# Attention ahead of routed experts: p times v by column tiles of 64 queries, four of seven key blocks in fp32, maxima in the tile shape of the scores, a new written order

## The chip, the cores and the metric

One core of a Trainium2 chip runs the whole kernel. The metric is the device time of one execution in microseconds, median of three runs. The core's engines are TensorE (PE, with its weight loads PEld), VectorE (DVE), ScalarE (ACT), GpSimd (POOL) and SyncE (SP), which here only issues transfers.

## The reference

Attention over 8 batches, 12 heads, 448 positions, 64 features, with normalized q and k, and then a two-level choice of one of 16 experts for each of the 3584 rows:

```python
q_n, k_n = (rmsnorm(q, g_q), rmsnorm(k, g_k))
scores = np.matmul(q_n, k_n.transpose(0, 1, 3, 2)) / np.sqrt(64)
attn = np.exp(scores - np.max(scores, axis=-1, keepdims=True))
attn = attn / (np.sum(attn, axis=-1, keepdims=True) + 1e-09)
attn_out = np.matmul(attn, v)
...
h = np.maximum(xg[mask_e] @ w1[g, e], 0.0)
ye = h @ w2[g, e]
out[tok_idx] = (g_w * e_w)[:, None] * ye
```

All inputs are fp32. The result must be nearly fp32, so the kernel splits most operands into a high and a low 16-bit part and adds three products (high by high, high by low, low by high).

## The kernel before

**Units.** The attention works on 24 units of four heads (8 batches, 3 units each). The four heads are two pairs: index r says which half of the partitions holds a head's 64 features, index i which half of the columns. A unit's 448 keys are seven blocks: for each i three blocks of 128 keys (0, 1, 2 for i = 0; 4, 5, 6 for i = 1), and block 3, in which the last 64 keys of both i lie one above the other.

**Steps of a unit.** `load` (line 206) brings k, q and v by transfers of SyncE's queue: q in two, k in four, v in six. `plan_prep` (236) squares (ACT), sums (DVE), takes the root and normalizes (POOL or DVE, line 281), transposes q and k on TensorE in fp32 (`tr`, 14 matmuls of 128x128, line 287), and splits them in high and low; for k the high part is taken away by a matmul in PSUM (`sub`, 305). `v_hi` and `v_lo` (320, 324) split v. `plan_max` (375) multiplies the high parts alone, seven times four matmuls of 64 features by 64 queries (line 384), and VectorE takes the row maximum of each (`rd`, 390, 128x896). The 14 columns of maxima are transposed (394), copied with a sign (398) and sent by two small transfers (403) into one row each of a tile `mr`. `plan_scores` (419) forms, for each of seven blocks, four products in PSUM, keys on the partitions: three of the high and low parts and, last, a matmul of a tile `one` with `mr` that takes the maximum away (433 for block 3 with tiles of 64x64, 437 with tiles of 64x128). ScalarE takes the exponential to fp32 p (444). `lo` (449) subtracts from p its upper 16 bits, which are read in place as bf16, and gives an fp16 rest `pl`; VectorE or GpSimd does it.

**Product with v.** `plan_av` (467) has p as the stationary operand, 128 keys by 128 queries, and v, with a 65th column that sums p, as the moving one (line 484). The queries of the two heads of one i are cut in eight pieces (`QUERIES`), one of them doubled where a head ends. For a block it runs three terms: p's upper half by `vh`, the same by `vl`, `pl` by `vh`: 24 matmuls of 65 or 64 columns. `FULL = (1,)` names the blocks that are done in one fp32 term instead (p by `vf`, 8 matmuls, which the trace shows as 16 passes); their p isn't split. Block 3 (`tails`) has 64 keys of each i and uses two row tiles. All add into one PSUM tile `po`, of which there is one. `norm` and `evac` (496 to 501, VectorE) divide, `plan_finish` splits the result (525, 528) and stores it in four transfers (537).

**Order.** Nothing is scheduled at run time: `Flow` (38) collects tasks with their engine, what they depend on and the buffers that they take; a written list `PLAN` (1402) gives each task its place in one order, and a star picks the second of two engines. Each engine obeys that order. `ROOM` (121) says how many buffers of a kind there are. Where `flow.shared` marks tasks, a VectorE task and the GpSimd task behind it are not let run at the same time (84 to 96): the GpSimd one waits.

**Around it.** The stored rows are routed in five groups (transposing transfers at 770, matmuls at 779, small steps to 860). The experts' matmuls (1239, 1266) begin when the attention is nearly done; their weights come by SyncE's queue in 768 KB pieces and are split by ACT and DVE (1179, 1181). Their buffers take the place of the attention's (`m2`, `m3`).

Of the kernel before, what the change touches and what calls it, by code (L numbers as in the profile page):

```python
# [12 lines left out]
F16 = mybir.dt.float16  # L13
BF16 = mybir.dt.bfloat16
# [23 lines left out]
class Flow:  # L38
# [3 lines left out]
    TURNS = ("n", "sq", "ss", "kh", "kl", "qh", "ql", "vf", "vh", "vl", "mx", "mxt", "mr", "po", "xm", "hl", "rx", *(f"st{i}" for i in range(8)), "gb0", "gb1")  # L42
# [65 lines left out]
FULL = (1,)  # L108
# [3 lines left out]
class Attention:  # L112
# [8 lines left out]
    ROOM = dict(n=2, sq=1, ss=1, kh=3, kl=2, qh=3, ql=3, vf=2, vh=2, vl=2, mx=2, mxt=2, mr=2,  # L121
# [3 lines left out]
    TILES = (3, 0, 1, 2, 4, 5, 6)  # L125
    FULL = FULL

    def __init__(self, tc, late, early, out, fin, q, k, v, g_q, g_k, x16):
# [17 lines left out]
        self.ident = t("ident", [P, P], F32)  # L146
        self.i16 = t("i16", [P, P], p=fin)
        self.one = t("one", [P, P])
        self.minus = t("minus", [P, P])
        self.vh = [t(f"vh{j}", [P, 14, 65]) for j in range(R["vh"])]  # L150
        self.pl = [t(f"pl{j}", [P, 2, 512]) for j in range(R["p"])]
        self.ln64 = t("ln64", [P, 1], F32)
        self.mr = [t(f"mr{j}", [P, self.W]) for j in range(R["mr"])]
        self.vf = [t(f"vf{j}", [P, 2, 7, 65], F32) for j in range(R["vf"])]
        self.p = [t(f"p{j}", [P, 2, 512], F32) for j in range(R["p"])]
# [6 lines left out]
    def init(self, j):  # L162
        nc, g = self.nc, self.nc.gpsimd
        f = lambda t: t.bitcast(F32)
        if j == 0:
            g.memset(self.eps, 64e-6 / 1024)
            make_identity(nc, self.ident)
            g.tensor_scalar(self.minus, self.ident, -1.0, None, op0=ALU.mult)
            g.memset(self.ln64, math.log(64.0))
# [3 lines left out]
        elif j == 1:  # L173
            o = self.one.bitcast(F32)
            g.memset(o, 0.0)
            for r in (0, 64):
                g.memset(o[r:r + 1], ONES)
            g.memset(f(self.mr[0]), 0.0)
        elif j == 2:
            g.memset(self.vf[0][:, :, :, 64:65], 1.0)  # L180
            g.memset(self.vh[0][:, :, 64:65], 64.0)
            for p, l in zip(self.p, self.pl):
                g.memset(p[:, 0, 448:512], 0.0)
                g.memset(l[:, 0, 448:512].bitcast(F32), 0.0)
            g.tensor_copy(self.i16, self.ident)
        else:
            for mr in self.mr[1:]:
                g.memset(f(mr), 0.0)
            for vf in self.vf[1:]:
                g.memset(vf[:, :, :, 64:65], 1.0)  # L190
# [15 lines left out]
    def load(self, u, nm, part=None, eng=None):  # L206
# [4 lines left out]
        s = dict(k=self.k, q=self.q, v=self.v)[nm][b, h0:h0 + self.HU].rearrange("(r i) t d -> i r t d", i=2)  # L211
        if nm == "v":
            t = d["v"] = self.vf[u % self.ROOM["vf"]][:, :, :, 0:64]
        else:
            if "n" not in d:
                d["n"] = self.nat.tile([P, 2, 2, 7, self.D], F32, tag="n", name=f"n{u}", bufs=self.ROOM["n"])
            t = d["n"][:, "kq".index(nm)]
# [6 lines left out]
        for i in range(2):  # L224
            if part in (None, i):
                x = s[i][:, 0:self.M].rearrange("r (p c) d -> p r c d", c=3)
                o = t[:, :, 4 * i:4 * i + 3]
                for r in range(2) if nm == "v" else ():
                    eng.dma_start(o[:, r], x[:, r])
# [1345 lines left out]
```

## Time and profile before

| | us |
|---|---|
| median of 3 runs (lowest, highest) | 982.34 (978.81, 988.64) |
| profiled execution | 982.85 |
| its span on the core | 981.2 |
| PE busy | 909.7 (93%) |
| PEld busy | 668.3 (68%) |
| DVE busy | 698.9 (71%) |
| ACT busy | 557.3 (57%) |
| POOL busy | 481.8 (49%) |

The shares are means over the whole span. The attention fills it from the start to about 465 us, the experts fill the rest, and the two have different limits, so the rows below are taken by stretch. A matmul's duration holds its way through the array, and matmuls overlap: what one costs in a stream is the time from its start to the next start. A weight load has its own row (PEld) and can run while earlier matmuls do. The notation 64*128 is the tile shape: rows of the array that are used by columns that are used.

### The profile page before, as it was taken

To read this page: it belongs to the slowest core of one execution; us is meant where nothing else is said; L and a number is where in the kernel's file an instruction comes from. 1 tells how busy PE (TensorE), PEld (TensorE's weight loads), DVE (VectorE), ACT (ScalarE), POOL (GpSimd) and SP (SyncE) were. 2 spreads that over 40 slices of the span, in tenths; PEclk is the share of its full clock that TensorE was granted. 3 is DMA by queue.
4 is the path that set the end of the run, shared out by engine and by line. 5 is a ranking of instruction groups with operands and counts; after the bars stand their busy time and mean duration, and the time that the engine had idled before them with its cause. 6 is when DMAs were issued, how large, how long until landed. Compare 5 with 4: busy or idle time off the path is not lost. (4 is left out here: it accounts for less than half of the span.)

```text
span 981.2 us, 29912 instructions
## 1 busy us (share of the span) xinstructions
PE 909.7 (93%) x12483; PEld 668.3 (68%) x12483; DVE 698.9 (71%) x824; ACT 557.3 (57%) x757; POOL 481.8 (49%) x519
## 2 busy tenths in 40 slices
PE   3899999999999989889989699899999999999996
PEld 1567667676666755557767576677877777788784
DVE  4899898989899987989562385575759455656540
ACT  3678677787766765665441364554646454555330
POOL 5586768786788685962343334133324123221211
PEclk9999999999999998999999799999999999999998
DMA  5334557566676765589998899998999699899510
GB/s 119 97 102 124 125 120 133 130 141 145 135 132 143 146 114 124 149 176 186 262 219 208 152 317 276 349 274 279 311 330 333 201 327 313 265 332 319 156 69 29
DMA packets 234301, 192.81 MB, mean 197 GB/s; under 512 B 156699, under 2 KB 197543, under 8 KB 234162
## 3 DMA queue, kind: packets, MB, share of 16 engines
q1 hardware_dynamic: 226002, 167.36, 65.9%
q0 software_dynamic: 7584, 23.04, 7.6%
q8 instruction: 99, 1.62, 0.7%
q10 hardware_dynamic: 576, 0.46, 0.2%
q14 instruction: 40, 0.33, 0.1%
HBM read 145.69 MB, written 23.41 MB: 172 GB/s over the span
## 5 line engine op out<-in xcount | busy, mean ns | idle before, releaser
L1239 PE MATMUL ps<-mx,w1h 128*128 128x256 f16 (+9 forms) x1728 | 239.9, 257 | 19.2 <-DVE hl L1248 15.9
L1239 PE MATMUL ps<-mx,w1l 128*128 128x256 f16 (+9 forms) x864 | 211.5, 257 | 0.0
L390 DVE TENSOR_REDUCE mx<-pmx 128x2 f32<-128x896 f32 x168 | 177.4, 1083 | 24.9 <-PE pmx L384 23.3
L449 POOL TENSOR_TENSOR pl<-p 128x896 f16<-128x896 f32 x94 | 157.0, 1684 | 62.1 <-DVE pl L449 25.1
L1239 PEld LDWEIGHTS <-w1h 128*128 128x128 f16 x1728 | 157.0, 100 | 33.5 <-issue 17.4
L1266 PE MATMUL ps<-w2h,hh 128*128 128x384 f16 (+2 forms) x768 | 163.8, 304 | 1.7 <-DVE y L1280 1.7
L1266 PE MATMUL ps<-w2l,hh 128*128 128x384 f16 (+2 forms) x768 | 163.8, 303 | 0.7 <-issue 0.7
L1266 PE MATMUL ps<-w2h,hl 128*128 128x384 f16 (+2 forms) x768 | 163.4, 303 | 0.0
L444 ACT ACTIVATE p<-pss 128x896 f32<-128x896 f32 x144 | 128.4, 917 | 61.0 <-PE pss L437 41.7
L1181 DVE SCALAR_TENSOR_TENSOR w1l<-stage,w1h 128x1536 f16<-128x1536 f32 x64 | 110.9, 1752 | 46.0 <-ACT w1h L1179 43.4
L1266 PEld LDWEIGHTS <-hh 128*128 128x128 f16 (+2 forms) x1536 | 101.5, 100 | 60.4 <-issue 7.5
L1248 DVE SCALAR_TENSOR_TENSOR hl<-ps,hh 128x256 f16<-128x256 f32 (+9 forms) x144 | 49.9, 368 | 110.0 <-ACT hh L1246 96.0
L484 PEld LDWEIGHTS <-p 128*128 128x128 bf16 (+1 forms) x2688 | 112.0, 98 | 22.0 <-issue 18.8
L1181 DVE SCALAR_TENSOR_TENSOR w2l<-stage,w2h 128x1536 f16<-128x1536 f32 x64 | 111.4, 1749 | 18.3 <-ACT w2h L1179 18.3
L1228 POOL DMA_INDIRECT xg<-x,tb x41 | 59.9, 1461 | 127.4 <-DMA mx<-xg 99.4
L484 PE MATMUL po<-vh,pl 128*128 128x65 f16 (+1 forms) x1344 | 117.6, 193 | 1.7 <-POOL pl L449 1.5
L484 PE MATMUL po<-vh,p 128*128 128x65 f16 (+1 forms) x1344 | 118.7, 195 | 0.4 <-issue 0.2
L484 PE MATMUL po<-vl,p 128*128 128x64 f16 (+1 forms) x1344 | 117.9, 192 | 0.0
L1179 ACT ACTIVATE w1h<-stage 128x1536 f16<-128x1536 f32 x64 | 92.7, 1478 | 34.4 <-DMA stage<-w 33.9
L1246 ACT ACTIVATE hh<-ps 128x256 f16<-128x256 f32 (+9 forms) x144 | 45.3, 343 | 116.6 <-PE ps L1239 70.2
L1179 ACT ACTIVATE w2h<-stage 128x1536 f16<-128x1536 f32 x64 | 93.7, 1479 | 29.9 <-DMA stage<-w 25.6
L1285 POOL DMA_INDIRECT out<-y,tb x21 | 34.8, 1658 | 152.7 <-ACT y L1278 70.2
(212 smaller groups left out, 1653.1 us busy)
## 6 DMA issues: line engine op xcount, KB each, us to landing
stage<-w SPq DMA_DIRECT2D x64, 768.0 KB
stage<-w SPq DMA_DIRECT2D x64, 512.0 KB
stage<-w SPq DMA_DIRECT2D x64, 256.0 KB
n<-q SPq DMA_DIRECT2D x46, 224.0 KB
n<-k SPq DMA_DIRECT2D x48, 192.0 KB
vf<-v SPq DMA_DIRECT2D x96, 96.0 KB
x<-xhl SPq DMA_DIRECT2D x48, 128.0 KB
x<-xhl SPq DMA_DIRECT2D x48, 96.0 KB
```

Of the source, the lines that this page charges most:

```text
L390: nc.vector.tensor_reduce(d["mx"][:, 2 * g:2 * g + 2], d.pop(("m", g))[:, :, 0:448], axis=AX.X, op=ALU.max)
L444: nc.scalar.activation(p[:, :, 0:448], d.pop(("s", g))[:, :, 0:448], AF.Exp, scale=1.0 / 64, **kw)
L449: ENG[eng].tensor_tensor(l[:, :, 0:448], p[:, :, 0:448], h, op=ALU.subtract)
L484: nc.tensor.matmul(po[:, i, 65 * G:65 * G + n], w, m, start=start and q + j == 0, stop=stop, skip_group_check=True)
L1179: self.nc.scalar.activation(hi, t, AF.Copy, scale=64.0)
L1181: self.nc.vector.scalar_tensor_tensor(lo, t, 64.0, hi, op0=ALU.mult, op1=ALU.subtract)
L1228: self.nc.gpsimd.indirect_dma_start(g[0:m], None, self.x16[0:n], bass.IndirectOffsetOnAxis(ap=tb[0:m, i, 0:1], axis=0), bounds_check=n - 1 ...
L1239: nc.tensor.matmul(s[:, 0:c], wb[w][:, i, fs], x[:, 2 * i + l, o:o + c], start=i + j == 0, stop=i == DC - 1 and j == 2)
L1246: self.nc.scalar.activation(hh, s[:, 0:c], AF.Relu)
L1248: self.nc.vector.scalar_tensor_tensor(hl, s[:, 0:c], 0.0, hh, op0=ALU.max, op1=ALU.subtract)
L1266: nc.tensor.matmul(s[q * m:q * m + m, 0:n], self.h[h][:, f, a:a + m], wb[w][:, f, o:o + n], start=f + j == 0, stop=f == self.FC - 1 and j ...
L1285: i = self.nc.gpsimd.indirect_dma_start(out, bass.IndirectOffsetOnAxis(ap=idx, axis=0), d.pop(("y", i))[:, 0:self.D // r], None, bounds_ch ...
```

## The change

- p by v with a stationary tile of 128 keys by 64 queries; the two heads of one i use the two halves of the array's columns, and of the PSUM partitions. `QUERIES` goes: seven pieces of 64 queries for each head.
- Blocks 3, 0, 1 and 5 are done in fp32 (`FULL`), with a v that is scaled by 64 in a new task `vone` (ACT or POOL, four operations a unit) into a tile `vo`, one buffer; the exponential has no bias for them any more. The order of the blocks is 3, 0, 4, 1, 5, 2, 6.
- Maxima of blocks of 128 queries with tiles of 64x128 (the last with 64x64), their transpose in two matmuls of 64 rows, `mxt` with one buffer; the columns of maxima lie beside the identity matrix.
- Transposes of q and k: 28 matmuls of 64 rows, each half of the partitions into a bank of its own.
- The matmul with the maxima is the first of the four in the scores.
- v and k come in three transfers each, the result goes in two. p's tiles are 448 wide, not 512, without padding to clear.
- `PLAN` is new. Read off it: subtractions `pl` on DVE 18 and on POOL 54 (before 50 and 94); normalizations on DVE 6, on POOL 40 (before 14 and 32, set-up's left out); `vone` on ACT 9, on POOL 15. Some small steps of the expert order are marked as shared.

```diff
-FULL = (1,)
+FULL = (3, 0, 1, 5)
...
-    ROOM = dict(n=2, ..., vl=2, mx=2, mxt=2, mr=2,
+    ROOM = dict(n=2, ..., vl=2, vo=1 if len(FULL) > 1 else 2, mx=2, mxt=1, mr=2,
...
-    TILES = (3, 0, 1, 2, 4, 5, 6)
+    TILES = (3, 0, 4, 1, 5, 2, 6)
...
         def tr(w, a, e):
-            t = d["t", w, a] = self.bank(f"pt{u}{w}{a}", W)
+            t = d["t", w, a] = self.pair(f"pt{u}{w}{a}")[:, :, 0:448]
...
             for g in range(a, e):
-                nc.tensor.matmul(t[:, g * P:g * P + P], n[:, g * P:g * P + P], self.ident, start=g in (a, 4), stop=w == 1,
-                                 is_transpose=True, skip_group_check=True)
+                for h in range(2):
+                    o = slice(64 * h, 64 * h + 64)
+                    nc.tensor.matmul(t[:, h, g * 64:g * 64 + 64], n[o, g * P:g * P + P], self.ident[o, o], start=g == a, stop=w == 1,
+                                     is_transpose=True, skip_group_check=True)
...
+        def v_one(eng):
+            d["vo"] = self.vo[u % self.ROOM["vo"]]
+            for j, g in enumerate(self.FULL):
+                o, x = d["vo"][:, j, :, 0:64], d["v"][:, :, g]
+                if eng == "ACT":
+                    nc.scalar.activation(o, x, AF.Copy, scale=64.0)
+                else:
+                    nc.gpsimd.tensor_scalar(o, x, 64.0, None, op0=ALU.mult)
...
     def plan_max(self, flow, u, B, D):
-            for i in range(2):
+            for i in range(2) if g == 6 else (g // 3,):
                 for r in range(2):
-                    h, o = slice(64 * r, 64 * r + 64), g * P + 64 * i
-                    nc.tensor.matmul(s[64 * i:64 * i + 64, r, 0:448], d["qh"][h, o:o + 64],
-                                     d["kh"][h, 448 * i:448 * i + 448], start=True, stop=True, skip_group_check=True)
+                    h = slice(64 * r, 64 * r + 64)
+                    o, n, w = (64 * i, 64, 448 * i + 384) if g == 6 else (0, P, 448 * i + g % 3 * P)
+                    nc.tensor.matmul(s[o:o + n, r, 0:448], d["qh"][h, w:w + n], d["kh"][h, 448 * i:448 * i + 448], **kw)
...
     def plan_scores(self, flow, u, B, D):
-            for j, (w, m) in enumerate(((d["kh"], d["qh"]), (d["kl"], d["qh"]), (d["kh"], d["ql"]), (None, d["mr"]))):
+            for j, (w, m) in enumerate(((self.one, d["mr"]), (d["kh"], d["qh"]), (d["kl"], d["qh"]), (d["kh"], d["ql"]))):
...
     def plan_av(self, flow, u, B, D):
         def run(g, heads, start=False, stop=False):
-            for q, (G, r, o) in enumerate(self.QUERIES):
-                for j, x in enumerate(zip(*(terms(g, rows, r, o) for _, rows in heads))):
-                    for (i, _), (w, m, n) in zip(heads, x):
-                        nc.tensor.matmul(po[:, i, 65 * G:65 * G + n], w, m, start=start and q + j == 0, stop=stop, skip_group_check=True)
+            for s in range(7):
+                x = [(i, r, terms(g, rows, r, s)) for i, rows in heads for r in range(2)]
+                for j in range(len(x[0][2])):
+                    for i, r, y in x:
+                        w, m, n = y[j]
+                        nc.tensor.matmul(po[self.HALVES[r], i, 65 * s:65 * s + n], w, m, start=start and s + j == 0, stop=stop, skip_group_check=True)
...
         def st():
+            for r, h in enumerate(self.HALVES):
+                nc.sync.dma_start(dst[:, :, 2 * (u % self.UB) + r], d["hl"][h].rearrange("p s l e -> p s (l e)"))
```

## Rows read from the trace of the kernel before

**Rows 1.** Windows by stage: start:end, length, busy us (count) per engine, PEclk, DMA.

```profile
40.00:465.00 425.00, 406.13 (x7375) 283.48 (x7374) 385.99 (x420) 303.19 (x419) 310.58 (x323) 0.98 0.62 135
...
560.00:960.00 400.00, 392.46 (x3905) 304.28 (x3894) 245.74 (x290) 201.07 (x254) 110.06 (x80) 1.00 0.90 276
```

**Rows 2.** Groups on VectorE, 40 to 465 us: count, busy us, mean ns, idle before.

```profile
L390 DVE TENSOR_REDUCE mx<-pmx 128x2 f32<-128x896 f32 x158 | 167.1, 1083 | 23.6 <-PE pmx L384 22.0
L449 DVE TENSOR_TENSOR pl<-p 128x896 f16<-128x896 f32 x50 | 57.5, 1176 | 0.2 <-ACT p L444 0.2
...
L281 DVE TENSOR_TENSOR sq<-n,z 128x896 f32<-128x896 f32 x14 | 15.5, 1107 | 0.5 <-POOL z L275 0.5
```

**Rows 3.** Groups on GpSimd, 40 to 465 us.

```profile
L449 POOL TENSOR_TENSOR pl<-p 128x896 f16<-128x896 f32 x93 | 155.4, 1684 | 54.7 <-DVE pl L449 25.1 <-DVE vl L324 5.9 <-ACT p L444 5.9
L281 POOL TENSOR_TENSOR sq<-n,z 128x896 f32<-128x896 f32 x30 | 50.8, 1700 | 3.6 <-DVE vl L324 1.3 <-DVE sq L281 1.1 <-PE pmx L384 0.3
```

**Rows 4.** Timeline of TensorE around 208 us: start us, duration us, instruction.

```profile
208.14 0.35 PE L437 MATMUL pss<-ql,kh 64*128 64x448 f16 x2
208.33 0.35 PE L437 MATMUL pss<-mr,one 64*128 64x448 f16 x2
208.61 0.38 PE L384 MATMUL pmx<-kh,qh 64*64 64x448 f16 x4
208.93 0.20 PE L484 MATMUL po<-vh,p 128*128 128x65 f16 x1
...
209.03 0.19 PE L484 MATMUL po<-vh,p 128*128 128x65 f16 x1
209.06 0.19 PE L484 MATMUL po<-vl,p 128*128 128x64 f16 x1
```

**Rows 5.** Timeline of TensorE in a tail (block 3).

```profile
214.48 0.19 PE L484 MATMUL po<-vl,p 64*128 64x64 f16 x2
214.51 0.19 PE L484 MATMUL po<-vh,pl 64*128 64x65 f16 x2
```

**Rows 6.** Timeline of one fp32 block: its passes, and its first two loads.

```profile
95.09 1.90 PE L484 MATMUL po<-vf,p 128*128 128x65 f32 x16
...
94.98 0.30 PEld L484 LDWEIGHTS po<-vf,p 128*128 128x128 f32 x2
```

**Rows 7.** Line 484 over the span: duration ns min/median/max.

```profile
L484 PEld LDWEIGHTS po<-vf,p x384: 186/192/193, 45.7 to 460.7; 128*128 128x128 f32 x192
L484 PE MATMUL po<-vf,p x384: 219/275/324, 45.8 to 460.8; 128*128 128x65 f32 x192
```

**Rows 8.** Column tiles in the experts: timeline of sets, and groups of loads.

```profile
538.04 0.26 PE L1266 MATMUL ps<-w2l,hh 128*32 128x192 f16 x4
538.12 0.26 PE L1266 MATMUL ps<-w2h,hl 128*32 128x192 f16 x4
...
L1266 PEld LDWEIGHTS <-hh 128*64 128x64 f16 x352 | 19.6, 111 | 12.3 <-issue 4.8
...
L1266 PEld LDWEIGHTS <-hh 128*32 128x32 f16 x448 | 10.5, 97 | 2.8 <-issue 2.7
```

**Rows 9.** Transposes of q and k: timeline of one unit, and durations in ns.

```profile
212.39 1.75 PE L287 MATMUL pt<-ident,sq 128*128 128x128 f32 x14
...
L287 PE MATMUL pt<-ident,sq x336: 271/273/475, 10.7 to 423.5; 128*128 128x128 f32 x168
```

**Rows 10.** Timeline of GpSimd: an operation of 140 columns.

```profile
379.57 0.44 POOL L793 TENSOR_TENSOR rd<-rl,rm 128x140 f32<-128x140 f32 x1 [3.75 <-DVE rm L791]
```

**Rows 11.** Timelines of SyncE's issues, and of TensorE at the largest hole.

```profile
330.82 2.65 SPq L537 DMA_DIRECT2D x<-xhl  x4
...
342.59 4.13 SPq L229 DMA_DIRECT2D vf<-v  x4
...
364.85 7.50 SPq L770 DMA_TRANSPOSE rx<-x  x2
...
369.16 0.20 PE L779 MATMUL prl<-wrh,rx 128*128 128x20 f16 x1 [2.92 <-DMA rx<-x]
```

More of the change, by code (lines that the diff above doesn't have):

```diff
@@ L297, in hi @@
             kw = dict(scale=self.ghc) if w else {}
-            nc.scalar.activation(d[nm][:, cols(a, e)], d["t", w, a][:, cols(a, e)], AF.Copy, **kw)
+            nc.scalar.activation(cols(d[nm], a, e, w), turned(w, a, e), AF.Copy, **kw)
         def sub(a, e):
-            t, h = d["t", 0, a], d["kh"]
-            for o, z in ((a * P, min(e, 4) * P), (4 * P, e * P)):
-                if a * P <= o < z:
-                    nc.tensor.matmul(t[:, o:z], self.minus, h[:, o:z], start=False, stop=True, skip_group_check=True)
+            for h in range(2):
+                nc.tensor.matmul(d["t", 0, a][:, h, a * 64:e * 64], self.minus, cols(d["kh"], a, e)[:, h],
+                                 start=False, stop=True, skip_group_check=True)
         def lo(w, a, e):
@@ L392, in fin0 @@
+        at = slice(96 - 96 * m, 110 - 96 * m)
         def fin0():
-            t = d["mt"] = self.bank(f"pmt{u}")
-            nc.tensor.transpose(t[0:14, 0:P], d["mx"], self.ident)
+            t = d["mt"] = self.pair(f"pmt{u}")
+            for j in range(2):
+                h = slice(64 * j, 64 * j + 64)
+                nc.tensor.matmul(t[:, j, 0:64], self.ix[h, 64 - 64 * m:192 - 64 * m], self.ident[h, h], start=True, stop=True, skip_group_check=True)
         def fin1():
-            d["mxt"] = self.wl.tile([14, P], F16, tag="mxt", name=f"mxt{u}", bufs=self.ROOM["mxt"])
@@ L530, in st @@
         def st():
-            for r in range(2):
-                f = dst[:, :, 2 * (u % self.UB) + r]
-                for j in range(2):
-                    G = slice(3 * r + (r and not j), 3 + 3 * r + (r or not j))
-                    n, s0 = G.stop - G.start, j if r == 0 else 1 - j
-                    nc.sync.dma_start(f[:, s0:s0 + 2 * n - 1:2], d["hl"][64 * j:64 * j + 64, G].rearrange("p g l e -> p g (l e)"))
+            for r, h in enumerate(self.HALVES):
+                nc.sync.dma_start(dst[:, :, 2 * (u % self.UB) + r], d["hl"][h].rearrange("p s l e -> p s (l e)"))
         x = flow.add("xhi", "ACT", hi, [D["x"]], takes=[B["hl"]], uses=[B["xm"]])
@@ L706, in turn @@
                 o = t[:, 0:S].rearrange("f (p s) -> f s p", s=7)
-                for k in range(3):
-                    nc.tensor.matmul(o[:, 2 * k + c:2 * k + c + 2], hl[:, 4 * c + k, l], self.i16, start=True, stop=True, skip_group_check=True)
-                h, s = slice(64 * c, 64 * c + 64), 0 if c else 6
-                nc.tensor.matmul(o[:, s:s + 1], hl[h, 3, l], self.i16[h, h], start=True, stop=True, skip_group_check=True)
+                h = slice(64 * c, 64 * c + 64)
+                for s in range(7):
+                    nc.tensor.matmul(o[:, s], hl[h, s, l], self.i16[h, h], start=True, stop=True, skip_group_check=True)
             def ev(eng, l, c):
```

382 lines of the change are left out of this document (197 added, 185 removed), and 39 rows, old and new, of the table PLAN.

## The prediction

> **What bounds the kernel now.** I read the windows by stage first, then the groups of VectorE and GpSimd in the attention stretch, then TensorE's timeline inside single units. The stretch from 40 to 465 us holds nearly all of the 24 attention units, 425 / 24 = 17.7 us each. TensorE has matmuls in flight for 406 of its 425 us and VectorE is busy for 386 (91%), ScalarE for 303, GpSimd for 311 [rows 1]. From 560 to 960 us the experts' matmuls run with TensorE at 392 of 400 us [rows 1]; the change leaves them alone, and the weights behind them are asked for only after the attention's routing is done. So what the attention stretch loses, the whole loses, and nothing is won elsewhere except by a better or worse hand-over between the two.
>
> In the attention stretch two engines are nearly full at once. VectorE's list is led by the 158 maxima (167 us), and 50 subtractions that split p into two fp16/bf16 parts cost it 57.5 us and 14 normalizations 15.5 us [rows 2]; GpSimd does the other 93 subtractions (155 us) and 30 normalizations [rows 3]. TensorE is read by start-to-start steps, since matmuls overlap. A set of score or maxima matmuls of 448 columns takes 0.19 us (208.14 to 208.33), and where the next set has another tile shape the step is 0.28 or 0.32: a change of shape costs about 0.1 us [rows 4]. Along the written order TensorE changes shape 316 times up to the last product with v, some 32 us.
>
> **The change part by part, per unit of four heads.**
>
> *Product of p and v, before.* A three-term block is 24 matmuls at a step of 0.03 us (209.03 to 209.06) [rows 4], 0.72; five of them are 3.6. The tail is 24 pairs of row tiles at the same 0.03 [rows 5], 0.72. The one fp32 block is 16 passes that last 1.90 us from the first start to the last end; less the 0.275 of the last, that is a step of 1.625 / 15 = 0.108, or 1.73 for the block [rows 6, 7]. Sum 6.05 us.
>
> *What the fp32 pass waits for.* Two of its weight loads lie 0.30 - 0.19 = 0.11 us apart [rows 6, 7], which is the step of the passes. Its matmuls last 219 ns where the weights were already there, 275 in the run of the block and 324 where nothing was loaded ahead [rows 7]. So the load of 128 fp32 columns (0.108) is the price, and the stream of 65 columns alone is shorter: a fp16 matmul of 65 columns shows 0.19 at a step of 0.03 [rows 4], the fp32 one with its weights there 0.03 more, so about 0.057.
>
> *After.* The stationary tile is 128 keys by 64 queries, in two column tiles side by side, so a three-term block is 42 matmuls or 21 pairs, a fp32 one 28 passes or 14 pairs, and the fp32 tail 14 quadruples (two row by two column tiles). A load of half the columns should take half, 0.054, and then load and stream are equal. If the two tiles of a pair run side by side, a fp32 block costs 14 x 0.058 = 0.81 us, and a three-term block 21 x 0.03 = 0.63. Four fp32 blocks (the tail among them) and three others: 3.25 + 1.89 = 5.14 us, 0.91 less than before. That column tiles do run side by side is seen in the experts: four tiles of 32 columns with 192 streamed columns go at 0.08 us a set (538.04 to 538.12), the time of one of them, with four weight loads in each set [rows 8]. A load of 64 columns lasts 111 ns against 97 for 32 [rows 8], so 64 take some 28 ns and stay under the 30 of the stream. Bounds: 5.14 if all of it is parallel, 9.9 or 8.2 in the rivals below. I take the low end, because the nearest rows are those of column tiles.
>
> *Transposes of q and k.* Before, 14 fp32 transposes at (1.75 - 0.273) / 13 = 0.11 us [rows 9], 1.54. After, 28 of 64 rows, two side by side in different banks, each streaming 64 columns rather than 128: 14 x 0.058 = 0.81 if the stream is what costs, 1.54 if it isn't. Their load is not the price: this step of 0.11 is what 128 columns of stream need at the 0.057 per 65 found above. I take 0.81, 0.73 less.
>
> *Maxima and scores.* The maxima become two matmuls of 128 queries by 64 features where there were four of 64, in the shape of the scores; a set still streams 448 columns, 0.19. The reduction on VectorE reads the same 896 columns (1.083) [rows 2]. Putting the row of the maxima first in each score set means that the first set of a unit waits for its small transfer before three steps that ran ahead of it; at most 3 x 0.19 = 0.57 us a unit, 14 us in all, and nothing where the transfer has landed. I take nothing, since sets of two units interleave in the order.
>
> *Changes of shape.* Maxima, scores and transposes now share 64x128, but p and v left 128x128, which the routing and the subtraction keep: counted along the new order 324 changes, 8 more, 0.8 us. I price the new pairs of shapes as the old ones.
>
> So TensorE loses 0.91 + 0.73 = 1.64 us a unit, 24 x 1.64 = 39 us.
>
> *VectorE and GpSimd.* The three further fp32 blocks need no split of p. The written order has 18 subtractions on VectorE and 54 on GpSimd, where it had 50 and 94; 6 normalizations on VectorE for 14. VectorE: 32 x 1.176 + 8 x 1.107 = 46.5 us less [rows 2], 386 to 340. GpSimd: 40 x 1.684 = 67 less, 8 normalizations x 1.70 = 14 more [rows 3], and the new scaling of v for the fp32 blocks, 15 units x 4 operations of 128 columns; a GpSimd operation of 140 columns takes 0.44 [rows 10], so at most 26: 311 to about 284. ScalarE takes the other 9 units, 9 x 4 at up to 0.44 = 16 on top of 303. Neither becomes the bound. The single buffer of scaled v makes the next unit's scaling wait for the fifth of seven blocks; at least nine TensorE tasks, four blocks of scores of 4 x 0.19 us among them, lie between there and its first use, over 3 us for four operations of 0.44. Uncovered it would be 1.8 us a unit.
>
> *Queue of SyncE.* Per unit it issues v in six transfers, four of which took 4.13 us here, and the stores in four that took 2.65 [rows 11]; after, v in three and the stores in two. The queue was not the bound over the stretch, but it made the largest hole: two transposing transfers held it from 364.85 for 7.5 us, and TensorE stood for the routing's x at 369.16 with 2.92 us idle [rows 11]. Fewer issues can only shorten that; I count nothing for it.
>
> *Sum.* TensorE gives up 39 us and VectorE 46, so the stretch can follow TensorE: 425 - 39 = 386, at which TensorE would have the same small slack as now and VectorE 340 / 386 = 88%. With 1 us for shapes and the set-up, the span falls from 981.2 to 942, and the profiled execution from 982.85 (0.5 us over the median of the three runs, 982.34) to 943. If TensorE is fed better because the other engines have more room, the 19 us of the stretch without matmuls can go too, 924 at best. If the slack grows instead, since four engines now lie between 284 and 386 us, I allow 20 us: 963.
>
> **The rivals.**
>
> *Loads of column tiles don't hide.* If a tile's load can't run beside the matmul of its neighbour in the same rows, a pair costs load plus stream: 0.058 in fp16, 0.111 in fp32, so 3 x 21 x 0.058 + 4 x 14 x 0.111 = 9.9 us, 3.8 more than before. With the transposes' 0.73 that is 3.1 x 24 = 74 us, about 1057. Against it stand the sets of four column tiles at 0.08, where four loads are hidden [rows 8]; for it, that none of those has fewer than 192 streamed columns to hide behind. The Trainium skill, page "TensorE: Matmul & The Clock Gate", Part 3, The mechanism, speaks for this rival: a weight load overlaps a running matmul only when its group of rows differs, and two column tiles have the same rows. By that rule the time is this rival's; the experts' sets disagree with it. Chance 0.07.
>
> *A fp32 pass has its price whatever its width.* If 0.11 belongs to the pass and not to its 128 columns, a block of 14 pairs costs 1.57 and the product 4 x 1.57 + 1.89 = 8.2 us, 2.1 more. Less 0.73 for the transposes, 1.4 x 24 = 33 us slower, 1016: slower than before from a price of 0.087 a pair on (4 x 14 x 0.087 + 1.89 + 0.81 = 7.6, the old sum). For it: every pass in the run of a block takes 0.108 to 0.112. Against it: the 219 and 324 ns matmuls, which only a load explains. Chance 0.07.
>
> *The engines are lighter, the order is not.* TensorE obeys one order; holes such as that at 362 to 372 us come from waits that no sum of loads shows. If new ones of that kind eat most of the 39 us, 966 to 990; and if the change doesn't make VectorE's work shorter where it counts, the time ends here too. For it: VectorE's idle 39 us of now. Chance 0.14.
>
> **How the numbers follow.** The forecast has 0.72, with its own 920 to 965 (924 and 963, and a little for what the set-up and the hand-over move). A run of this kernel can tell about 1% from no change, 973 to 993. Faster by over 1%: 0.72 and a third of the third rival, 0.77. Within: 0.08. Slower: the first two rivals and a remainder, 0.15. The range must leave out no more than 0.2: 920 to 985 leaves the first two rivals, the end of the third and what is below 920.
>
> **What would show it.** Right: fp32 matmuls of 128x64 at 0.06 us a pair; three-term pairs at 0.03; transposes two in 0.06; VectorE's subtractions down to 18 and its busy time in the attention stretch near 340; the last product with v near 425 us instead of 465, and about 516 us from there to the end as now. Wrong: fp32 pairs at 0.11 or fp16 pairs at 0.06; a stretch that stays at 425 us with VectorE idle for far more than 50; or an end that doesn't follow because the hand-over to the experts waits longer.

## The result and the profile after

The changed kernel takes 949.47 us, median of 4 runs (947.49 to 949.95), beside 982.91 for the kernel before: ratio 0.9652 [0.9601, 0.9703]. In a later session, beside other runs of the kernel before (976.82), it took 938.78 us (935.21 to 946.12), ratio 0.9596 [0.9546, 0.9646]. The forecast of 943 is 0.959 of the profiled 982.85. The two runs lie on both sides of it, one 6.5 us above and one 4 below. The kernel before took 6 us less in the later session too, so the ratios compare the two better than the times.

Where the span of the profiled execution went:

| us | before | after | after, second profile |
|---|---|---|---|
| first evacuation of the attention starts | 55.4 | 54.1 | 54.6 |
| last evacuation starts | 465.1 | 438.7 | 430.3 |
| from there to the end of the span | 516.1 | 508.4 | 514.2 |
| span | 981.2 | 947.1 | 944.5 |

So the attention gave 26.4 us in the first profile and 34.8 in the second, where 39 were forecast, and 7.7 and 1.9 us came behind it, where nothing was forecast. The row of the attention stretch, window view of the changed kernel (columns as in [rows 1]):

```profile
40.00:439.00 399.00, 378.98 (x9408) 261.38 (x9405) 336.70 (x380) 307.60 (x447) 294.12 (x346) 0.99 0.64 142
```

Read it against the first row of [rows 1]: TensorE in flight for 379 us instead of 406, VectorE 337 instead of 386 (forecast 340), ScalarE 308 instead of 303, GpSimd 294 instead of 311 (forecast 284).

TensorE's timeline of the changed kernel, three places: a three-term block with the set of maxima ahead of it, one fp32 block, one transposed tensor (start us, duration us, instruction).

```profile
111.22 0.74 PE L410 MATMUL pmx<-kh,qh 64*128 64x448 f16 x6
111.89 0.22 PE L518 MATMUL po<-vh,p 128*64 128x65 f16 x2
111.95 0.20 PE L518 MATMUL po<-vl,p 128*64 128x64 f16 x2
111.98 0.20 PE L518 MATMUL po<-vh,pl 128*64 128x65 f16 x2
...
112.55 0.20 PE L518 MATMUL po<-vh,pl 128*64 128x65 f16 x2
...
208.27 1.04 PE L518 MATMUL po<-vo,p 128*64 128x65 f32 x28
...
219.31 0.61 PE L290 MATMUL pt<-ident,sq 64*128 64x64 f32 x14
```

Each fp16 row is a pair ("x2": one tile of 64 queries per half of the columns of the array), and a pair starts every (112.55 - 111.98) / 18 = 0.032 us. In [rows 4] that was the step of one matmul of 128 queries. The fp32 block runs from 208.27 to 209.31; less the last matmul's 0.22 it is 0.82 us for 13 steps of a pair, 0.063; the first of them takes 0.107, the others 0.058 each. Seven pairs of transposes take 0.61 - 0.22 = 0.39 us, less 0.02 by which the second matmul of a pair starts behind the first, for 6 steps: 0.061. That the loads stay beside the stream is seen in line 518 over the whole span (duration ns, min/median/max):

```profile
L518 PEld LDWEIGHTS po<-vo,p x3360: 129/138/140, 38.4 to 433.6; 128*64 128x64 f32 x119, 64*64 64x64 f32 x79
L518 PE MATMUL po<-vo,p x3360: 217/222/273, 38.4 to 433.7; 128*64 128x65 f32 x119, 64*64 64x65 f32 x79
```

The median fp32 matmul now lasts 222 ns, what [rows 7] showed as the least, "weights already there"; 275 was the median before, when each waited for its load.

VectorE and GpSimd, groups of the stretch 40 to 439 us (count, busy us, mean ns, idle before):

```profile
L415 DVE TENSOR_REDUCE ident<-pmx 128x2 f32<-128x896 f32 x157 | 166.3, 1086 | 33.7 <-PE pmx L410 32.7
...
L483 DVE TENSOR_TENSOR pl<-p 128x896 f16<-128x896 f32 x18 | 21.7, 1214 | 0.5 <-ACT p L478 0.5
...
L281 DVE TENSOR_TENSOR sq<-n,z 128x896 f32<-128x896 f32 x6 | 6.5, 1088 | 0.0
```

GpSimd's groups of the same stretch:

```profile
L483 POOL TENSOR_TENSOR pl<-p 128x896 f16<-128x896 f32 x54 | 92.2, 1712 | 36.2 <-DVE vl L333 13.0 <-ACT p L478 8.9 <-DVE pl L483 5.6
...
L343 POOL TENSOR_SCALAR vo<-v 128x128 f32<-128x128 f32 x60 | 34.2, 592 | 2.1 <-PE po L518 2.0
```

These answer to [rows 2, 3]: the maxima cost what they did, the subtractions on VectorE fell from 50 to 18 and the normalizations from 14 to 6. The scaling of v costs GpSimd 0.592 us an operation, where I had taken 0.44 as the most.

What the forecast did not have is in TensorE's timeline beside routing stores, in the first of the two profiles only:

```profile
346.16 0.20 PE L518 MATMUL po<-vh,pl 128*64 128x65 f16 x2
346.19 0.20 PE L518 MATMUL po<-vh,p 128*64 128x65 f16 x2
346.63 0.22 PE L518 MATMUL po<-vl,p 128*64 128x64 f16 x2 [0.23 <-issue]
346.67 0.22 PE L518 MATMUL po<-vh,pl 128*64 128x65 f16 x2
347.36 0.24 PE L518 MATMUL po<-vh,p 128*64 128x65 f16 x2 [0.48 <-issue]
347.40 0.23 PE L518 MATMUL po<-vl,p 128*64 128x64 f16 x2
348.12 0.24 PE L518 MATMUL po<-vh,pl 128*64 128x65 f16 x2 [0.49 <-issue]
```

GpSimd's timeline at the same time:

```profile
343.42 1.70 POOL L483 TENSOR_TENSOR pl<-p 128x896 f16<-128x896 f32 x1
345.28 0.99 POOL L874 DMA_INDIRECT tab<-row,slot  x1 [0.17 <-issue]
346.58 0.98 POOL L874 DMA_INDIRECT tab<-row,slot  x1 [0.30 <-issue]
347.86 0.97 POOL L874 DMA_INDIRECT tab<-row,slot  x1 [0.30 <-issue]
```

In the middle of a block, four matmuls (two rows of a pair each) and their four loads start, then nothing for 0.7 us, and again, one group every 0.76 us. The trace shows nothing that is waited for ("issue"). The view of waits sums it up (us in total, times, longest). TensorE at line 518 in the first profile, 40 to 438 us:

```profile
PE po L518 <- issue: 8.9, 15, 2.6
```

And in the second, 40 to 430 us:

```profile
PE po L518 <- issue: 1.7, 3, 0.8
```

The second profile is of the same program in the later session (its run of 946.12 us, the longest of its four); its last evacuation starts at 430.27, not at 438.68.

A second thing that the forecast did not have is TensorE's granted clock. In the first profile it stood at half (1.2 GHz) right behind two of the three places with such steps, from 349.8 to 353.2 and from 387.4 to 390.8 us. The window row of the first (columns as in [rows 1], the clock is the 0.50), and two pairs of a block in it:

```profile
349.80:353.20 3.40, 3.40 (x93) 2.51 (x89) 2.17 (x3) 1.92 (x8) 0.00 (x0) 0.50 0.47 44
```

```profile
351.42 0.25 PE L518 MATMUL po<-vh,pl 128*64 128x65 f16 x2
...
352.40 0.25 PE L518 MATMUL po<-vh,pl 128*64 128x65 f16 x2
```

A pair starts every (352.40 - 351.42) / 18 = 0.054 us there, and every 0.032 at the full 2.4 GHz. From 40 us to the last evacuation the clock was at half for 13.6 us in the kernel before (361.6 to 365.0, 368.4 to 375.2, around the hole of [rows 11], and 429.8 to 433.2), for 6.9 in the first profile and for none of it in the second. By the two steps that cost some 5, 3 and 0 us: up to 5 of the second profile's 34.8 us are the clock's and not the lighter engines'.

### The profile page after: what moved, and what is told of

Read it like the earlier page. It is cut to its first block, busy times and chain, and to the rows that moved or that the text cites. A ratio compares the mean times of both kernels' runs of the same rounds, so it can differ in the third digit from the quotient of the medians.

```text
span 947.1 us, 33908 instructions
## 1 busy us (share of the span) xinstructions
PE 879.8 (93%) x14585; PEld 644.4 (68%) x14585; DVE 653.8 (69%) x785; ACT 565.2 (60%) x792; POOL 446.5 (47%) x535
## 5 line engine op out<-in xcount | busy, mean ns | idle before, releaser
L415 DVE TENSOR_REDUCE ident<-pmx 128x2 f32<-128x896 f32 x168 | 177.7, 1086 | 34.9 <-PE pmx L410 33.7
L478 ACT ACTIVATE p<-pss 128x896 f32<-128x896 f32 x168 | 148.0, 916 | 45.7 <-PE pss L472 41.1
L1257 POOL DMA_INDIRECT xg<-x,tb x41 | 52.5, 1282 | 165.3 <-DMA mx<-xg 124.8
L483 POOL TENSOR_TENSOR pl<-p 128x896 f16<-128x896 f32 x54 | 92.2, 1712 | 36.2 <-DVE vl L333 13.0
L518 PEld LDWEIGHTS po<-vo,p 128*64 128x64 f32 (+1 forms) x3360 | 86.7, 136 | 17.8 <-issue 14.2
L518 PE MATMUL po<-vo,p 128*64 128x65 f32 (+1 forms) x3360 | 97.2, 223 | 1.1 <-issue 0.9
L1268 PEld LDWEIGHTS <-w1l 128*128 128x128 f16 x864 | 85.1, 99 | 5.4
L1314 POOL DMA_INDIRECT out<-y,tb x21 | 28.0, 1332 | 122.5 <-ACT y L1307 62.6
L281 POOL TENSOR_TENSOR sq<-n,z 128x896 f32<-128x896 f32 (+2 forms) x43 | 70.2, 1648 | 13.2 <-ACT rl L812 5.1
```

The lines of the kernel that those rows point to most:

```text
L281: ENG[eng].tensor_tensor(o, x, z.unsqueeze(3).to_broadcast([P, 2, e - a, self.D]), op=ALU.mult)
L415: nc.vector.tensor_reduce(o, d.pop(("m", g))[:, :, 0:448], axis=AX.X, op=ALU.max)
L478: nc.scalar.activation(p, d.pop(("s", g))[:, :, 0:448], AF.Exp, scale=1.0 / 64)
L483: ENG[eng].tensor_tensor(l, p, h, op=ALU.subtract)
L518: nc.tensor.matmul(po[self.HALVES[r], i, 65 * s:65 * s + n], w, m, start=start and s + j == 0, stop=stop, skip_group_check=True)
L1257: self.nc.gpsimd.indirect_dma_start(g[0:m], None, self.x16[0:n], bass.IndirectOffsetOnAxis(ap=tb[0:m, i, 0:1], axis=0), bounds_check=n - 1 ...
```

## The experiments

The theories. A: TensorE's steps set the attention stretch. B: VectorE sets it. C: both do, and either alone gives part. F1: the indirect stores of the routing (GpSimd, line 874) cut the feed of TensorE's instructions; F2: the larger number of instructions does; F3: it takes something that only some chips or loadings have.

The measures are the start of the last evacuation ("last"), and the shares of the time from 40 us to there in which TensorE and VectorE were busy, by the window view. The whole times of two runs say little, as told there. The clock was at half for 10.2 us of that stretch in the first fp32 version, for 17.1 in the stores twice and in the kernel before without the fp32 block (alone and with both edits), for 7 or less in the other edits, which by the steps above is up to some 7 us, so differences of a few us between two runs carry little.

| run | time us | ratio to before | last us | PE | DVE |
|---|---|---|---|---|---|
| before | 982.91 | | 465.1 | 0.956 | 0.908 |
| changed kernel | 949.47 | 0.9652 [0.9601, 0.9703] | 438.7 | 0.950 | 0.844 |
| changed, again | 938.78 | 0.9596 [0.9546, 0.9646] | 430.3 | 0.957 | 0.862 |
| transposes twice | 959.89 | 0.9827 [0.9755, 0.9899] | 445.7 | 0.966 | 0.830 |
| two maxima twice | 975.64 | 0.9982 [0.9946, 1.0018] | 465.5 | 0.895 | 0.895 |
| no stores | 932.29 | 0.9555 [0.9477, 0.9634] | 427.0 | 0.970 | 0.864 |
| no low part of v | 935.96 | 0.9572 [0.9504, 0.9639] | 422.8 | 0.943 | 0.866 |
| before, no fp32 block | 1053.45 | 1.0760 [1.0688, 1.0831] | 463.7 | 0.875 | 0.907 |
| before, short subtractions | 970.37 | 0.9932 [0.9896, 0.9968] | 456.1 | 0.972 | 0.848 |
| before, both | 1044.50 | 1.0721 [1.0648, 1.0794] | 451.2 | 0.901 | 0.855 |
| all blocks fp32 | 964.04 | 0.9847 [0.9808, 0.9886] | 449.6 | 0.952 | 0.720 |
| all fp32, more on GpSimd | 961.06 | 0.9807 [0.9775, 0.9838] | 448.9 | 0.951 | 0.699 |
| maxima last | 950.94 | 0.9715 [0.9674, 0.9756] | 438.3 | 0.951 | 0.843 |
| stores twice | 966.48 | 0.9896 [0.9874, 0.9918] | 456.0 | 0.913 | 0.823 |

The runs were taken in five sessions, each on one chip with runs of the kernel before beside it (the changed kernel; transposes twice to no low part of v; the changed kernel again and the three edits of the kernel before; both fp32 versions and the maxima last; the stores twice). So ratios are compared, not times.

**Transposes twice** (changed kernel, line 289):

```diff
-            for g in range(a, e):
+            for g in [*range(a, e), *range(a, e)]:
```

> The changed kernel with the transposes of q and k issued twice into the same banks (the second pass writes the same values): 14 pairs more per transposed tensor at 0.062 us, 0.87 us of TensorE per tensor and 1.7 per unit, and nothing for any other engine. Theory A (the stretch follows TensorE's own steps): 48 x 0.87 = 42 us, less what falls into holes where TensorE waits anyway (about 30 us of them in the stretch), so 25 to 42 us longer, 975 to 991 us. Theory B (VectorE and the waits set the stretch, TensorE has room): under 8 us, at most 958.

The expectation counted the pairs twice over: a tensor has 14 matmuls, 7 pairs, so the second pass is 336 pairs, 21 us and not 42. By the matmuls' steps it measured some 19 us. The last evacuation came 7.0 us later than in the first profile of the changed kernel and 15.4 later than in the second, in which, as here, the steps of 0.7 us are missing. Against the second, 15 of 19 us is A: in the new order a microsecond more on TensorE is most of a microsecond more of the stretch. Against the first alone, 7.0 us would be B's.

**Two maxima twice** (line 415):

```diff
-            nc.vector.tensor_reduce(o, d.pop(("m", g))[:, :, 0:448], axis=AX.X, op=ALU.max)
+            s = d.pop(("m", g))[:, :, 0:448]
+            for _ in range(2 if g in (1, 4) else 1):
+                nc.vector.tensor_reduce(o, s, axis=AX.X, op=ALU.max)
```

> The changed kernel with two of the seven maxima of a unit reduced twice (same input, same output): 48 x 1.086 = 52 us of VectorE, 337 to 389 in the attention stretch, which is what it had in the kernel before; TensorE's work is unchanged. Theory A (TensorE's steps alone set the stretch, VectorE's relief was spare): under 8 us longer, at most 958. Theory B (the gain needed both reliefs): 20 to 50 us longer, 970 to 1000, with VectorE at over 93% of the stretch.

A fails: the last evacuation is back at 465.5 and the whole gain is gone, though TensorE's work is that of the changed kernel. TensorE's waits (40 to 430 us) name the place: the sets of scores and maxima wait for PSUM banks that a reduction still reads.

```profile
PE pss L472 <- DVE ident L417: 16.6, 23, 1.3
PE pmx L410 <- DVE ident L417: 11.6, 14, 2.1
```

VectorE was busy for 0.895 of the stretch, not over 93%. It was 0.908 in the kernel before and 0.907 there without the fp32 block; no run here shows more. The edit also holds two of a unit's seven banks 1.1 us longer; no run separates that from VectorE's load.

**Before, with one or both reliefs.** The edits to the kernel before: (1) the task of the fp32 block issues nothing, (2) three of six subtractions of p handle 8 columns (and `pl` is cleared once at the start).

```diff
         def main(i, c):
+            if 4 * i + c in self.FULL:
+                return
...
-            ENG[eng].tensor_tensor(l[:, :, 0:448], p[:, :, 0:448], h, op=ALU.subtract)
+            n = 8 if g in (2, 4, 5) else 448
+            ENG[eng].tensor_tensor(l[:, :, 0:n], p[:, :, 0:n], h[:, :, 0:n], op=ALU.subtract)
```

> The kernel before without its one fp32 block (leaves out the product of that key block with v): 16 passes, 1.73 us a unit, 41.5 us of TensorE less, all other engines as before. Theory A (TensorE's steps set the stretch): 35 to 42 us shorter, 0.957 to 0.965 of the time before. Theory B (VectorE sets it): less than 10 us, over 0.99. Theory C (both are bounds, and either alone gives part): 10 to 30 us.

> The kernel before with the subtractions of three key blocks cut to 8 of 448 columns (leaves out p's low part there; TensorE still multiplies a tile of old values): 32 subtractions less on VectorE, 32 x 1.18 = 38 us, and 40 less on GpSimd, 67 us; TensorE's work is as before. Theory A: under 6 us shorter. Theory B: 20 to 38 us, 0.961 to 0.98. Theory C: 5 to 20 us.

> The kernel before with both edits: TensorE loses 41.5 us and VectorE 38, about what the change takes from each (39 and 46). Theory A: as without the fp32 block alone, 35 to 42 us. Theory B: as with the short subtractions alone. Theory C: the sum of both or more, 35 to 42 us, though neither alone gave it.

Without a key block the attention's output differs and so does the routing: the experts' first product has 2880 matmuls in these two runs and 2592 in all others, so their whole times do not count, and the last evacuation does. The window row of the stretch for (1):

```profile
40.00:463.70 423.70, 370.54 (x7003) 245.66 (x7000) 384.11 (x422) 303.53 (x420) 311.62 (x323) 0.98 0.62 136
```

For (2):

```profile
40.00:456.10 416.10, 404.58 (x7397) 282.53 (x7394) 352.73 (x422) 304.93 (x421) 251.93 (x324) 0.99 0.62 139
```

For both edits:

```profile
40.00:451.20 411.20, 370.52 (x7005) 246.04 (x7006) 351.60 (x422) 303.78 (x421) 251.06 (x324) 0.98 0.63 140
```

TensorE lighter by 41 us (by the step of 0.108; in flight 36 less) gave 1.4 us, which is B's, with VectorE at 0.907 as before. VectorE lighter by 33 (and GpSimd by 59) gave 9.0, which is C's, and then TensorE stood at 0.972. Both gave 13.9, which no theory had (A and C 35 to 42): neither engine is full (0.901 and 0.855). What TensorE waits for instead (both reliefs, 40 to 430 us):

```profile
PE pt L305 <- ACT kh L298: 11.5, 11, 2.1
PE pmx L384 <- DVE mx L390: 6.9, 8, 1.9
PE pmx L384 <- ACT kh L298: 6.5, 5, 1.5
```

The first of these lines was 2.7 us in the kernel before (40 to 465 us). The old order puts the subtraction of k's high part (line 305) a little behind the transposes of k, and ScalarE's copy of kh must come between. In 13 of the 22 units whose transposes lie behind 40 us it was the fp32 block that TensorE did meanwhile. One of them, in the kernel before:

```profile
77.93 0.96 PE L287 MATMUL pt<-ident,sq 128*128 128x128 f32 x7
78.72 1.90 PE L484 MATMUL po<-vf,p 128*128 128x65 f32 x16
80.46 0.54 PE L305 MATMUL pt<-kh,minus 128*128 128x512 f16 x2
```

The same place with both edits:

```profile
78.48 0.96 PE L287 MATMUL pt<-ident,sq 128*128 128x128 f32 x7
80.44 0.54 PE L305 MATMUL pt<-kh,minus 128*128 128x512 f16 x2 [1.00 <-ACT kh L298]
```

So part of what edit (1) took from TensorE came back as a wait, because it took the work from the place that covered that copy. With nearly the same reliefs the changed kernel gains 26 to 35 us, and this wait is 0.2 us there (first profile, 40 to 439 us). Its order was written for these reliefs, but its buffers, transfers and tile shapes differ too, so how much of the rest is the order's is not shown.

**All blocks in fp32.** The splits of p and v fall away with their places in the written order (120 of 2941), and v is scaled by one operation a unit. The second version moves normalizations, splits of x and the scaling of v to GpSimd.

```diff
-FULL = (3, 0, 1, 5)
+FULL = (0, 1, 2, 3, 4, 5, 6)
...
-            if g not in self.FULL:
-                x = flow.shared(flow.add("pl", ["POOL", "DVE"], ...
```

> The changed kernel with all seven key blocks in fp32, so that no split of p or v is left; the written order is the same less the tasks that fall away, and v is scaled by one operation per unit. TensorE: three blocks of 14 pairs at 0.058 in place of 21 at 0.032 us, 0.14 us more each, 72 x 0.14 = 10 us more. VectorE: 18 subtractions of p at 1.21 and 24 of v at 1.20 fewer, 50 us less; GpSimd 92 us less; ScalarE some 20 less. Theory A (TensorE sets the stretch): 6 to 10 us slower than the changed kernel, 0.967 to 0.972 of the time before. Theory C (TensorE and VectorE both, through waits for VectorE's reductions): 8 to 25 us faster than it, 0.935 to 0.955.

> As all blocks in fp32, and what GpSimd then has room for moved to it: 6 normalizations and 5 splits of x from VectorE (11 x 1.09 = 12 us), the scaling of v from ScalarE. VectorE at 275 of some 380 us, GpSimd at about 240. Theory C: 2 to 8 us faster than with all blocks in fp32 alone; Theory A: the same within 2 us.

The window row of the first version:

```profile
40.00:449.60 409.60, 389.82 (x8413) 271.38 (x8401) 294.91 (x340) 289.07 (x402) 201.09 (x249) 0.99 0.60 138
```

A, and more than A: VectorE has 42 us less to do and the last evacuation comes 11 us later than in the first profile of the changed kernel, 19 later than in the second. TensorE's matmuls, by their steps, need some 11 us more (expected: 10), and TensorE is at 0.952. With VectorE at 0.720 relief on it is worth nothing any more, nor is the further relief of the second version. So in the changed kernel more work on TensorE costs most of its length, and VectorE is close behind: 44 us more of it (337 to 381 by the window view) took 27 to 35. Less work on TensorE gives less: see the run without the low part of v below.

**Maxima last** (lines 463 to 472): the row of the maxima goes to the fourth step.

```diff
-            for j, (w, m) in enumerate(((self.one, d["mr"]), (d["kh"], d["qh"]), (d["kl"], d["qh"]), (d["kh"], d["ql"]))):
+            for j, (w, m) in enumerate(((d["kh"], d["qh"]), (d["kl"], d["qh"]), (d["kh"], d["ql"]), (self.one, d["mr"]))):
```

> The changed kernel with the row of the maxima last in each score set, as before the change (four steps, the row's at the end; start and stop flags follow the order). If its first place costs (a unit's first set waits for the small transfer before three steps that could run ahead): 3 to 10 us faster than the changed kernel, 0.95 to 0.957 of the time before. If the transfer has landed by then, as I predicted (0.3 us of waiting for it in the second profile): the same within 3 us.

The last evacuation starts at 438.3 beside 438.7, and the ratio, 0.9715, is no lower than the changed kernel's: the first place costs nothing, as I had taken it. The profile also showed the steps of 0.7 us again, at 342 to 349 and 385 to 388 us.

**The steps of 0.7 us.** Four runs bear on them: without the stores, without the low part of v, the changed kernel again, and with every store issued a second time into a table that nobody reads.

```diff
             self.listed += 1
+            return
```

> The changed kernel without the indirect stores by which GpSimd lists the tokens of each expert (this leaves out the lists: the experts then work on padding rows, in the same number). Theory F1 (the indirect stores, whose descriptors GpSimd writes, slow the feed of TensorE's instructions: the steps of 0.6 to 0.7 us inside the products with v at 342 to 350 us and 385 to 389 us lie beside them): these steps go, and the last evacuation comes 6 to 10 us earlier than 438.7 us. Theory F2 (the feed fails because the products have many more instructions now): steps of 0.6 to 0.7 us stay in number, and the last evacuation moves by less than 3 us.

```diff
-            return [(h, d["vh"][rows, n], 65), (h, d["vl"][rows, n], 64), (l[rows, r, q], d["vh"][rows, n], 65)]
+            return [(h, d["vh"][rows, n], 65), (l[rows, r, q], d["vh"][rows, n], 65)]
```

> The changed kernel without the product of p's high part with v's low part (leaves out one of the three terms in the three-term blocks): 14 of 42 matmuls and loads of a block, so 7 pairs of 0.032 us, 0.22 us a block, 24 x 3 x 0.22 = 16 us of TensorE. Theory A alone: 12 to 16 us shorter, 934 to 938 us. Theory F2 (the number of instructions starves the feed): the steps of 0.6 to 0.7 us inside the products go as well, some 10 us more, 922 to 928. Theory F1: the steps at 340 to 390 us stay where the indirect stores are.

> The changed kernel itself once more, unedited, on the chip of these runs. If the steps of 0.6 to 0.7 us inside the products with v at 342 to 350 and 385 to 389 us belong to the program (its order and where its instructions lie), they come again at the same places, 13 us in all from the first to the last evacuation; if they belong to one execution, they are elsewhere or gone and the last evacuation comes up to 10 us earlier than 438.7 us.

```diff
-            i = nc.gpsimd.indirect_dma_start(
-                self.tab, ...
+            for to, puts in ((self.tab, "puts"), (self.tab2, "puts2")):
+                i = nc.gpsimd.indirect_dma_start(
+                    to, ...
```

> The changed kernel with every indirect store of the token lists issued a second time into a table of its own that nobody reads: some 31 us of such stores more on GpSimd up to the last evacuation, which has room for them (294 of 399 us), and a few more behind it in the routing's tail. Theory F1 (such a store, where it runs beside products with v, can cut TensorE's feed to 8 instructions per 0.76 us): in this profile the steps of 0.4 to 0.8 us without a wait lie beside the stores again, and there are more than the 8 to 12 that the changed kernel showed, 15 to 25 of them, 10 to 17 us. Theory F3 (it needs something that only some chips or loadings have, and stores alone do nothing): few or none, as in the second profile of the changed kernel, and a last evacuation near 431 to 436 us. Both: the whole is 5 to 20 us slower than the changed kernel by the routing's tail.

Without the stores the steps beside them were gone, and the last evacuation came 11.7 us earlier, more than F1's 6 to 10. Four steps of 0.8 to 1.7 us without a wait stayed at other places, two of them (63 and 119 us) where the first profile of the changed kernel has one too. The unedited kernel in the later session took the finding back: its stores run beside as many products, no step lies beside them, and it ends the attention 8.4 us earlier. I counted, in each profile, steps of over 0.4 us from one product to the next, without a wait, that lie beside a store: 12 in the changed kernel, 8 with the maxima last, 7 and 9 in the two fp32 versions, and none in the second profile, with the transposes twice, the maxima twice, the low part of v left out, or the stores twice. The four that show them are of two sessions; all others that have stores, of three other sessions, show none. Stores alone don't do it (F1 fails), nor does the number of instructions (F2: the fp32 versions have fewer in their products, 10752 matmuls and loads against 12768, and show them); 36 of the 44 such steps in these four profiles lie beside stores. F3 is what remains, by exclusion. One execution of each program was profiled in a session, so whether it is the chip, the loading or the single execution is open.

The run without the low part of v is some 16 us lighter on TensorE by its steps and ended the attention 15.9 us before the first profile, 7.5 before the second. Its time lies in A's 934 to 938, but the later sessions are faster for the kernel before as well, and by ratio (0.9572) it is 8 us below the first run of the changed kernel and 2 below the second. Like the second profile it has no step beside a store: against that one, TensorE's relief gave half of its length. It is not F2's 922 to 928.

The stores twice cost 17 us in the attention over the first profile where F3 expected none, by another way; by ratio the whole is 24 to 29 us slower, where 5 to 20 were expected. GpSimd's timeline:

```profile
354.06 0.97 POOL L875 DMA_INDIRECT tab<-row,slot  x1 [0.30 <-issue]
355.34 0.97 POOL L875 DMA_INDIRECT tab<-row,slot  x1 [0.30 <-issue]
356.33 1.70 POOL L483 TENSOR_TENSOR pl<-p 128x896 f16<-128x896 f32 x1
```

TensorE at the end of that split:

```profile
358.08 0.27 PE L518 MATMUL po<-vh,pl 128*64 128x65 f16 x2 [4.36 <-POOL pl L483]
```

A split of p stands on GpSimd's queue behind stores that come every 1.28 us, and TensorE waits 4.36 us for it. The longest wait comes by a second way, some 50 us later. VectorE's timeline:

```profile
406.90 0.41 DVE L987 TENSOR_REDUCE oof<-pick 1x16 f32<-1x256 f32 x1 [9.78 <-POOL pick L985]
407.24 1.07 DVE L415 TENSOR_REDUCE ident<-pmx 128x2 f32<-128x896 f32 x1
```

And TensorE's:

```profile
408.36 0.56 PE L470 MATMUL pss<-mr,one 64*128 64x448 f16 x2 [9.73 <-DVE ident L415]
```

A small operation of the expert order stands on GpSimd's queue behind ten stores, VectorE waits 9.78 us for it in its own fixed order, the next maximum comes after that, and TensorE waits 9.73 us. Its share of the stretch falls to 0.913. GpSimd has room by its sum, 319 of 416 us, and not at those places.

No version here is shown to beat the changed kernel; the two that are shorter leave work out.

## Why the prediction was right

**The sum.** TensorE was forecast to give up 0.91 + 0.73 a unit, 39 us, less 0.8 for changes of shape. Adding up the steps of all matmuls of the stretch, kind by kind, with the changes of shape, gives about 394 us before, 359 after and 358 in the second profile: 35. The product with v fell from 147.7 to 126.5 us, 0.88 a unit; the transposes from 34.1 to 19.4 over the 22 units whose transposes lie in the stretch, 0.67 a unit. The fp32 pair at 0.058 and the fp16 pair at 0.032 stand (0.058 and 0.03 forecast); the pair of transposes at 0.061 is 0.003 dearer. Two things were missing or wrong in the sum. The maxima's transposes, now two of 64 rows for one, take 2.6 us more in all and were counted at nothing. And the changes of shape, counted 8 up, are 347 before and 313 after in the traces' shapes, about 33 and 31 us. VectorE fell by 49 us (46.5 forecast).

**The rivals on the product.** Loads that don't hide would have shown pairs at 0.058 and 0.111, a price per pass would have shown 0.11; both are off the table by the steps of line 518. The Trainium skill, page "TensorE: Matmul & The Clock Gate", Part 3, The mechanism, has in one sentence that weight loads overlap a running matmul only where the group of rows differs. The pairs contradict it: both tiles have the same 128 rows, and their loads cost nothing at a step of 0.032 us for two loads and two matmuls. The kernel before contradicted it already: each 128x128 matmul of [rows 4] has its own load on the same 128 rows (line 484: 2880 fp16 matmuls of this shape and 2880 loads) and starts 0.03 us behind the last, so this rival could have been dropped ahead of the run. One reading of mine against it doesn't hold: I took from loads of 111 and 97 ns that a fp16 load of 64 columns takes some 28. The view that has these rows shows loads of 128 columns (line 484) at 98 and 99 ns, so the difference is no price by the column.

**"So the stretch can follow TensorE."** True, but the reason given, that TensorE gives up 39 us and VectorE 46, is not enough. Nearly the same reliefs in the old order gave 14 us, not 39. The two sums had to fall, since either alone gave 1 and 9, and the work had to go from places where it covers no other engine's step, or something else had to cover it. The share that I gave to "the engines are lighter, the order is not" was right to be there; why it did not come true is in part shown (the wait for ScalarE's copy of kh, 11.5 us with both edits and 0.2 in the changed kernel). The rest I put down to the new order, whose worth I had not worked out and which no run here measures by itself.

**"TensorE would have the same small slack as now."** What the stretch holds beside the steps and the changes of shape is 31 us before, 40 in the first profile and 32 in the second. It held in the second profile by luck: some 5 of the 31 were the half clock, which the second profile hasn't, so the waits proper grew by about as much. In the first profile the steps without a wait inside the products hold some 11 us. This is the term that was mis-sized for that execution. Nothing in the trace of before shows them: no step of over 0.4 us without a wait stands between its products.

**"About 516 us from there to the end as now."** 516.1 before, 508.4 and 514.2 after; over all runs with 2592 matmuls it lies between 501 and 516.5. In the first profile TensorE waits 5.7 us for VectorE's hidden values (470 to 570 us), 12.0 before (500 to 600 us), and its clock was at half for 10.1 us there (up to 40 us before the end), 17.1 before and 20.5 in the second profile. The two ends of the range go the same way: 3.4 us at half clock in the run of 501.0 (without stores), 23.9 in that of 516.5 (stores twice). These 7.7 us made up for most of what the attention fell short in the first profile. That was luck, for the prediction had no reason for them: with its 516 behind the last evacuation that execution would have taken about 957.

**Two edits counted at nothing.** The row of the maxima first: nothing, measured by the run that undoes it. The scaling of v on GpSimd: 34 us, where I had 26 as the most, and hidden, for TensorE's longest waits (40 to 439 us) show none of it.

## What to carry to other kernels

When two engines are nearly full and tied through a few buffers, relief on one is worth little, and relief on both is worth what the order of issue lets through; look for the share that each engine reaches when it is the bound (here 0.95 to 0.97 for TensorE and 0.90 for VectorE), and where neither is there after the change, look at the order. Before work is taken from an engine, look at what runs under it: the fp32 block that edit (1) left out had covered a copy on ScalarE. Halving the width of stationary tiles and running two side by side cost next to nothing here in fp16 (0.032 us a pair for 0.03 a matmul) and nearly halved the price of fp32 (0.058 for 0.108). Profile a result in more than one session, and look at the granted clock of the stretch, before putting a difference of 1% down to the program.

## What the runs showed of the hardware that was not expected

A stream of short matmuls with a load for each (a three-term block is 42 of both in some 0.7 us) ran, at times, at four matmuls and four loads per 0.76 us for several groups in a row, with no wait in the trace and mostly beside GpSimd's indirect stores. The same program showed it in one session (three such stretches, and a single step of 2.84 us without a wait up to 437 us) and not in another (three single steps of 0.6 to 1.0 us), and the attention ended 8.4 us apart. What brings it is open. The kernel before has no such step between its products.
